# Results of a chunk kept in one piece of TensorE's order, between the halves of the next chunk's scores

## The chip, the cores and the metric

The kernel runs on one core of a Trainium2 chip. The metric is the device time of one execution in microseconds; lower is better. Before the change the median of three runs is 552.49 us (552.18 to 552.93).

Names of the engines in the profile: PE is TensorE (PEld its loading of weights), DVE is VectorE, ACT is ScalarE, POOL is GpSimd, SP issues most of the transfers. All of them run their own list of instructions in order and wait for each other by semaphores.

## What is computed

A gated linear recurrence with a complex decay for each of 4 x 8 heads (768 steps, head dimension 48), then a mixture of eight experts, one expert for each of the 3072 rows:

```python
for t in range(S):                                   # S = 768
    ar, ai = a_re_n[:, :, t, :, None], a_im_n[:, :, t, :, None]
    new_re = ar * S_re - ai * S_im
    new_im = ar * S_im + ai * S_re
    kv = np.einsum('bhd,bhe->bhde', k[:, :, t], v[:, :, t])
    S_re, S_im = new_re + kv, new_im
    y[:, :, t] = np.einsum('bhd,bhde->bhe', q[:, :, t], S_re)
# [...] x = y as (3072, 384) rows
expert_idx = np.argmax(x @ w_gate, axis=1)
# [...] gate weight by softmax; rows sorted by expert
h = np.maximum(x_sorted[lo:hi] @ w1[e], 0.0)         # 384 -> 1024
y_sorted[lo:hi] = h @ w2[e]                          # 1024 -> 384
```

## The kernel before

The recurrence is done in chunks of 128 steps: one chunk `g` is 128 steps of all eight heads of one batch entry, so there are 24 chunks, four (the batch entries `b`) for each of six stretches `s` of the sequence. Two chunks form a unit `u`. For each unit the decays are summed along the steps by a matmul with a triangle (`csl` for the logarithm of the magnitude, `cst` for the angle), turned into factors on ScalarE and VectorE, and multiplied into q and k. Real and imaginary part stand side by side, so q and k of a head have 96 columns. Then, for each chunk:

- `tp`: TensorE transposes q and k, four heads at a time; copies bring them to SBUF as `qt` and `kt`.
- `at`: the scores k times q, 128 x 128 for each head, four heads in one PSUM bank; VectorE multiplies them with the triangle into `am`.
- `dk`: k times v, what the chunk adds to the state.
- `y`: the results, v with the scores plus the state `G` with q. Heads come in pairs: `z = 0` writes partitions 0 to 63, `z = 1` partitions 64 to 127.
- `tpx`, `lt`, `lp`: the results are transposed back and the router's logits are made from them.

```python
psT = ...tile_pool(name="psT", bufs=2, space=PSUM)   # tp
psA = ...tile_pool(name="psA", bufs=1, space=PSUM)   # at
psY = ...tile_pool(name="psY", bufs=1, space=PSUM)   # y
# [...]
def scores(g):

    u, c = divmod(g, U)
    s, b = divmod(g, B)
    Q, K = rotated(u, c, "Q"), rotated(u, c, "K")      # VectorE
    qts, ats = [], []
    for hg in range(H // 4):
        kq = []
        for nm, X in (("qt", Q), ("kt", K)):
            tp = psT.tile([P, 4, P], FP, tag="tp", name="tp")
            for j in range(4):
                nc.tensor.transpose(out=tp[0:DD, j], in_=X[:, hg * 4 + j], identity=ident)
            t = ch.tile([P, 4, P], FP, tag=nm, name=nm, bufs=4 if nm == "qt" else 2)
            copy(nm == "qt" or hg == 1, t[0:DD], tp[0:DD])   # True: ScalarE, False: VectorE
            kq.append(t)
        at = psA.tile([P, 4, P], FP, tag="at", name="at")
        for j in range(4):
            mm(at[:, j], kq[1][0:DD, j], kq[0][0:DD, j])
        am = ch.tile([P, 4, P], FP, tag="am", name="am", bufs=4)
        nc.vector.tensor_tensor(out=am, in0=at, in1=bc(tri, 1, 4), op=OP.mult)
        # [...]
    if s < CB - 1:
        dk = psD.tile([P, H, D], FP, tag="dk", padded_shape=[P, 8, 64], name="dk")
        for h in range(H):
            mm(dk[0:DD, h], K[:, h], T["v", u][:, c, h, 0:D])

def outputs(g):
    # [...]
    y = psY.tile([P, HP, P], FP, tag="y", name="y")
    for i in range(HP):
        for z in range(2):
            hg, j = divmod(2 * i + z, 4)
            mm(y[z * DP : (z + 1) * DP, i], V[:, 2 * i + z], ats[hg][:, j], True, s == 0)
        if s > 0:
            for z in range(2):
                hg, j = divmod(2 * i + z, 4)
                mm(y[z * DP : (z + 1) * DP, i], G[0:DD, 2 * i + z], qts[hg][0:DD, j], False, True)
    # [...] state: t = dk + G on VectorE, G = t * M once in four chunks
    xt = xl.tile([P, HP, P], FP, tag="xt", name="xt")
    nc.scalar.copy(out=xt, in_=y)
    tp = psB.tile([P, HP, 2, DP], FP, tag="tp", name="tpx")
    for i in range(HP):
        nc.tensor.transpose(out=tp[:, i].rearrange("p z d -> p (z d)"), in_=xt[:, i], identity=ident)
    # [...] copy to x on ScalarE
    logits(xt, g)                                      # lt, copy ls, lp, copy lg
```

The loop, with the decay steps of the next unit left out:

```python
for u in range(NU + 1):
    # [...] loads; decay_steps, decay_sums (csl), angle_sums (cst), rotation (CS)
    for c in range(U):
        g = (u - 1) * U + c
        if g >= 0:
            scores(g)
        if u < NU:
            decayed(u, c)
        if g > 0:
            outputs(g - 1)
        # [...] routing of chunks that are done
```

The order of this text is not the order on the engines. A scheduler places each instruction, within what data and buffers allow; only instructions tied with `queue(...)` keep their order for certain. In `before` nothing ties the matmuls of the chunks. All matmuls work in f32; TensorE takes each in two passes, which the trace records as two instructions.

After the 24th chunk the expert part begins: for each expert `hps` (384 to 1024) and `yps` (1024 to 384), with the weights loaded ahead.

Of the kernel before, what the change touches and what calls it, by code (L numbers as in the profile page):

```python
# [10 lines left out]
FP = mybir.dt.float32  # L11
# [3 lines left out]
OP = mybir.AluOpType  # L15
# [5 lines left out]
P = 128  # L21
# [8 lines left out]
def bc(ap, axis, n):  # L30

    shape = list(ap.shape)
    shape.insert(axis, n)
    return ap[tuple([slice(None)] * axis + [None])].to_broadcast(shape)
# [3 lines left out]
def kernel(  # L38
# [12 lines left out]
    nc = tc.nc  # L51
    B, H, S, D = q.shape
    DD = 2 * D
# [4 lines left out]
    NT = N // P  # L58
    CB = S // P
    U = 2  # L60
# [14 lines left out]
    DP = 64  # L75
    HP = H // 2
# [3 lines left out]
    def mm(o, lhsT, rhs, start=True, stop=True):  # L80
        return nc.tensor.matmul(o, lhsT=lhsT, rhs=rhs, start=start, stop=stop, skip_group_check=True)  # L81

    def copy(i, o, in_):
        (nc.scalar.copy if i % 2 else nc.vector.tensor_copy)(out=o, in_=in_)  # L84
# [7 lines left out]
    def const(shape, name, dt=FP):  # L92
        return cp.tile(shape, dt, name=name)

    ident = const([P, P], "ident")
    make_identity(nc, ident)
    tri = const([P, P], "tri")
# [21 lines left out]
    gbuf = [const([P, H, DP], f"G{i}") for i in range(B)]  # L119
# [39 lines left out]
    T, W_T = {"put": []}, {}  # L159

    def queue(ins, before):

        tc.add_manual_dep(ins.ins, before.ins.name, NOSYNC, reason="queue order")
        return ins
# [55 lines left out]
    ch = att.enter_context(tc.tile_pool(name="ch", bufs=2))  # L220
    psM = att.enter_context(tc.tile_pool(name="psM", bufs=1, space=PSUM))
    psT = att.enter_context(tc.tile_pool(name="psT", bufs=2, space=PSUM))
    psA = att.enter_context(tc.tile_pool(name="psA", bufs=1, space=PSUM))
    psY = att.enter_context(tc.tile_pool(name="psY", bufs=1, space=PSUM))
    psB = att.enter_context(tc.tile_pool(name="psB", bufs=1, space=PSUM))
    psD = att.enter_context(tc.tile_pool(name="psD", bufs=1, space=PSUM))
# [47 lines left out]
    def load_a(u):  # L274
        load(u, (("ar", a_re), ("ai", a_im)))
# [131 lines left out]
    def rotated(u, c, nm):  # L407
        t = ch.tile([P, H, 2, D], FP, tag=nm, name=nm)
        e = bc(T.pop((nm, u, c)), 2, 2)
        nc.vector.tensor_tensor(out=t, in0=T["CS", u][:, c * H : (c + 1) * H], in1=e, op=OP.mult)  # L410
        return t.rearrange("p h a d -> p h (a d)")
# [78 lines left out]

        return [lambda i=i: put(i) for i in range(n)] + ([last] if end else [])

    def scores(g):

        u, c = divmod(g, U)
        s, b = divmod(g, B)
        Q, K = rotated(u, c, "Q"), rotated(u, c, "K")
        qts, ats = [], []
        for hg in range(H // 4):
            kq = []  # L500
            for nm, X in (("qt", Q), ("kt", K)):
                tp = psT.tile([P, 4, P], FP, tag="tp", name="tp")
                for j in range(4):
                    nc.tensor.transpose(out=tp[0:DD, j], in_=X[:, hg * 4 + j], identity=ident)  # L504
                t = ch.tile([P, 4, P], FP, tag=nm, name=nm, bufs=4 if nm == "qt" else 2)
                copy(nm == "qt" or hg == 1, t[0:DD], tp[0:DD])
                kq.append(t)
            at = psA.tile([P, 4, P], FP, tag="at", name="at")
            for j in range(4):
                mm(at[:, j], kq[1][0:DD, j], kq[0][0:DD, j])  # L510
            am = ch.tile([P, 4, P], FP, tag="am", name="am", bufs=4)
            nc.vector.tensor_tensor(out=am, in0=at, in1=bc(tri, 1, 4), op=OP.mult)  # L512
            qts.append(kq[0])
            ats.append(am)
        if s < CB - 1:
            dk = psD.tile([P, H, D], FP, tag="dk", padded_shape=[P, 8, 64], name="dk")
            for h in range(H):
                mm(dk[0:DD, h], K[:, h], T["v", u][:, c, h, 0:D])
            T["dk", g] = dk
        T["s", g] = qts, ats  # L520

    def outputs(g):

        u, c = divmod(g, U)
        s, b = divmod(g, B)
        qts, ats = T.pop(("s", g))
        V, G = T["v", u][:, c], gbuf[b]
        y = psY.tile([P, HP, P], FP, tag="y", name="y")
        for i in range(HP):
            for z in range(2):  # L530
                hg, j = divmod(2 * i + z, 4)
                mm(y[z * DP : (z + 1) * DP, i], V[:, 2 * i + z], ats[hg][:, j], True, s == 0)
            if s > 0:
                for z in range(2):
                    hg, j = divmod(2 * i + z, 4)
                    mm(y[z * DP : (z + 1) * DP, i], G[0:DD, 2 * i + z], qts[hg][0:DD, j], False, True)
        if s < CB - 1:
            t = ch.tile([P, H, D], FP, tag="t", name="t")
            if s == 0:
                nc.scalar.copy(out=t[0:DD], in_=T["dk", g][0:DD])  # L540
            else:
                nc.vector.tensor_tensor(out=t[0:DD], in0=T["dk", g][0:DD], in1=G[0:DD, :, 0:D], op=OP.add)
            if b == B - 1:
                decay_total(s)
            T["t", b] = t
            if b == B - 1:
                for i in range(B):
                    M = bc(T["M", s][0:DD, i], 2, D)
                    (nc.vector.tensor_tensor(out=gbuf[i][0:DD, :, 0:D], in0=T["t", i][0:DD], in1=M, op=OP.mult))
# [5 lines that stand above are left out]
        if b == 0:  # L555
            T["x", g] = T["x"] = xl.tile([P, GR, XW], FP, tag="x", name="x", bufs=3)
        T["copied"] = nc.scalar.copy(
            out=T["x"][:, b, :DM].rearrange("p (i z d) -> p i z d", z=2, d=D), in_=tp[:, :, :, 0:D]
        )
        logits(xt, g)  # L560
# [24 lines left out]
    for z in range(2):  # L585
        nc.sync.dma_start(
            out=wg[z * DP : z * DP + D, :, 0:E],
            in_=w_gate.rearrange("(i z d) e -> z d i e", z=2, d=D)[z],
# [14 lines left out]
    for u in range(NU + 1):  # L603
        if 0 < u < NU:
            load_qkv(u)
        for i in range(NS // (P * BL)):
            if 2 + i * 2 // (NS // (P * BL)) == u:
                blank(i)

        if u < NU:  # L610
            steps = decay_steps(u + 1)[0] if u + 1 < NU else []
            own = [lambda c=c: decay_sums(u, c) for c in range(U)]
            if u == 0:
                steps = steps[:2] + own + steps[2:]
            else:
                steps = steps[:1] + own[:1] + steps[1:3] + own[1:] + steps[3:]
            table("natural_log_exp_and_others")
            for i, f in enumerate(steps):
                f()
                if i == 1:  # L620
                    carry_angle(u)
            for f in T.pop("chosen", []):
                f()
            for c in range(U):
                angle_sums(u, c)
            table("trig_and_small")
            if 0 < u < NU - 1:
                decay_angle(u + 1)
            rotation(u)
            if u == 0:  # L630
                decay_angle(1)
            if u == NU - 1:
                while T["put"]:
                    place()
                experts_at(range(1), True)
                load_w(0, range(KD + KF // 2))
                own0 = gather(0, 0, [P] * (FIRST // P))
        if u < NU:
            place()
        for f in T.pop("route", []):  # L640
            T["put"] += f()
        for c in range(U):
            g = (u - 1) * U + c
            if g >= 0:
                scores(g)
            if u < NU:
                decayed(u, c)
            if g > 0:
                outputs(g - 1)

            n = {NT - GR: GR, NT - U: U}.get(g)
            if n:
                if n == GR:
                    queue(table("natural_log_exp_and_others"), T["copied"])
                choose(g - n, n)()
                T["put"] += route(g - n, n)
                while T["put"]:
                    place()
        for _ in range(2 if u >= NU - 2 else 1):
            place()  # L660
        if u > 2 and u % 2 and u < NU - 1:

            j = (u - 3) * U
            T["chosen"] = [choose(j, GR)]
            T["route"] = [lambda j=j: route(j, GR)]
        if u + 2 < NU:
            load_a(u + 2)
    outputs(NT - 1)
    choose(NT - U, U)()
    for f in route(NT - U, U):  # L670
# [343 lines left out]
```

## Time and profile before

| | before |
|---|---|
| time, median of three | 552.49 us |
| span of the profiled execution | 551.8 us |
| TensorE busy | 535.6 us (97%) |
| VectorE busy | 272.0 us (49%) |
| ScalarE busy | 279.7 us (51%) |
| GpSimd busy | 128.5 us (23%) |
| read from and written to HBM | 63.3 and 15.5 MB, 143 GB/s |

The page gives busy time over the whole span, and then the span in 40 slices of 13.8 us, one digit each (tenths of the slice). Chunks run up to about 278 us, which is slice 20; what follows is the expert part. For what happens inside the first half three other views are used: stages of 20 us, the waits of one engine (who waited for whom, total, times, longest), and the timeline, where each line is a group of neighbouring instructions with start, length, engine, line of the code, output and inputs, and the number of records. Neighbouring matmuls overlap in the timeline, so the length of a group is longer than the time to the next group's start.

The costs of the instructions concerned, from the groups between 0 and 320 us (number of records, mean length of one):

| instruction | records | mean |
|---|---|---|
| `at`, TensorE | 384 | 286 ns |
| `y` from `am` and v, TensorE | 384 | 288 ns |
| `y` from `qt` and G, TensorE | 320 | 280 ns |
| `tp` of q and of k, TensorE | 192 each | 285, 283 ns |
| `dk`, TensorE | 320 | 252 ns |
| copy to `qt`, ScalarE | 48 | 581 ns |
| copy to `kt`, VectorE / ScalarE | 24 / 24 | 683 / 581 ns |
| `am`, VectorE | 48 | 687 ns |
| `xt`, ScalarE | 24 | 587 ns |

### The profile page before, as it was taken

What the parts mean: (1) busy time and instruction counts of PE and PEld (TensorE: products, weight loads), DVE (VectorE), ACT (ScalarE), POOL (GpSimd) and SP (SyncE); (2) the same over time, 40 slices, a digit from 0 to 9 for tenths busy, and PEclk for the clock granted to TensorE, in tenths of its full rate; (3) what the DMA queues carried; (4) which work ended last, traced back from release to release, by engine and by line L of the source; (5) the groups of instructions that cost most, each with busy time, mean ns of one, the idle gap of its engine ahead of it and who ended that gap; (6) DMA issues with size and microseconds to landing.
All of it is one profiled execution on the core that took longest, in us unless ns stands there. A gap on an engine that the chain in (4) does not pass through costs nothing.

```text
span 551.8 us, 8779 instructions
## 1 busy us (share of the span) xinstructions
PE 535.6 (97%) x3310; PEld 369.7 (67%) x3310; DVE 272.0 (49%) x640; ACT 279.7 (51%) x473; POOL 128.5 (23%) x148
## 2 busy tenths in 40 slices
PE   8899999999999999999999999999999999999995
PEld 6777688778778878778776655555555555565553
DVE  3757788978888887877551212121404032210110
ACT  7867877877776886744310112534343351615200
POOL 2110111141241140210222000605234160514301
PEclk9959999999999999999999999999999999999998
DMA  9999954918754633461114996472944819370001
GB/s 186 187 259 236 262 94 88 182 52 145 129 131 88 121 84 58 105 224 18 43 44 113 309 359 160 136 194 121 281 137 163 240 47 280 128 255 15 25 4 42
DMA packets 163566, 79.32 MB, mean 144 GB/s; under 512 B 144896, under 2 KB 156861, under 8 KB 162619
## 3 DMA queue, kind: packets, MB, share of 16 engines
q1 hardware_dynamic: 158651, 69.04, 51.6%
q0 software_dynamic: 4864, 9.63, 5.0%
q8 instruction: 28, 0.46, 0.4%
q14 instruction: 23, 0.19, 0.1%
HBM read 63.30 MB, written 15.46 MB: 143 GB/s over the span
## 4 chain that ended last, share of the span: by engine, by line
PE 84%; DMA 6%; DVE 3%; ACT 3%; issue 3%; SPq 0%; POOL 0%; POOLq 0%; DVEq 0%; ACTq 0%
PE hps L81 23%; PE yps L81 22%; PE y L81 9%; PE at L81 7%; PE tp L504 7%; PE dk L81 5%; PE cst L81 3%; PE csl L81 3%; DMA ai<-in_a_im_dram 2%; PE tpx L554 2%; DMA xs<-x,slot 1%; PE lt L81 1%; DMA ai<-c 1%; DMA c<-ai 1%; ACT R L230 1%
## 5 line engine op out<-in xcount | busy, mean ns | idle before, releaser
L81 PE MATMUL yps<-w2t,ht 128*128 128x384 f32 (+6 forms) x464 | 135.1, 487 | 0.0
L81 PE MATMUL hps<-xt,w1t 128*128 128x256 f32 (+8 forms) x432 | 133.9, 469 | 0.3 <-DVE xt L708 0.3
L81 PEld LDWEIGHTS hps<-xt,w1t 128*128 128x128 f32 x432 | 80.0, 190 | 52.8 <-issue 25.2
L81 PEld LDWEIGHTS yps<-w2t,ht 128*128 128x128 f32 (+6 forms) x464 | 75.8, 177 | 56.8 <-issue 6.9
L742 ACT ACTIVATE ht<-hps 128x256 f32<-128x256 f32 (+8 forms) x36 | 17.0, 472 | 118.5 <-PE hps L81 117.5
L759 DVE TENSOR_SCALAR y<-yps,gi 128x384 f32<-128x384 f32 (+2 forms) x24 | 14.7, 615 | 107.6 <-PE yps L81 107.6
L722 POOL DMA_INDIRECT out_dram<-y,gi x29 | 28.2, 974 | 122.6 <-DVE y L759 86.5
L81 PE MATMUL at<-qt,kt 96*128 96x128 f32 x384 | 54.9, 286 | 0.9 <-DVE kt L84 0.9
L746 DVE TENSOR_SCALAR ht<-hps 128x256 f32<-128x256 f32 (+8 forms) x36 | 19.2, 532 | 70.9 <-PE hps L81 70.8
L81 PEld LDWEIGHTS at<-qt,kt 96*128 96x128 f32 x384 | 48.7, 196 | 6.5 <-DVE kt L84 1.4
L81 PE MATMUL y<-am,v 128*64 128x128 f32 x384 | 52.8, 288 | 0.0
L81 PE MATMUL y<-qt,G 96*64 96x128 f32 x320 | 45.5, 280 | 0.0
L482 POOL DMA_INDIRECT xs<-x,slot x24 | 24.8, 1035 | 86.2 <-DMA xs<-x,slot 39.8
L81 PEld LDWEIGHTS y<-am,v 128*64 128x64 f32 x384 | 32.7, 137 | 13.7 <-issue 12.3
L512 DVE TENSOR_TENSOR am<-at,tri 128x512 f32<-128x512 f32 x48 | 33.0, 687 | 13.9 <-PE at L81 13.4
L84 ACT COPY qt<-tp 96x512 f32<-96x512 f32 x48 | 27.9, 581 | 15.1 <-PE tp L504 15.0
L242 ACT ACT_TABLE_LOAD x27 | 34.6, 1283 | 1.2 <-PEq L1000 0.8
L504 PE MATMUL tp<-ident,Q 128*96 128x128 f32 x192 | 32.5, 285 | 2.0 <-DVE Q L410 2.0
L800 POOL TENSOR_TENSOR cs<-cs,cw 128x768 f32<-128x768 f32 x12 | 21.7, 1809 | 50.7 <-ACT cw L796 50.7
L81 PEld LDWEIGHTS dk<-v,K 128*96 128x96 f32 x320 | 31.4, 170 | 3.0 <-issue 1.9
L504 PE MATMUL tp<-ident,K 128*96 128x128 f32 x192 | 32.5, 283 | 0.7 <-DVE K L410 0.7
L81 PEld LDWEIGHTS y<-qt,G 96*64 96x64 f32 x320 | 30.9, 136 | 3.2 <-issue 2.6
(140 smaller groups left out, 752.8 us busy)
## 6 DMA issues: line engine op xcount, KB each, us to landing
w1t<-in_moe_w_dram SPq DMA_DIRECT2D x7, 1536.0 KB, 7.1
w2t<-in_moe_w_dram SPq DMA_DIRECT2D x7, 1536.0 KB, 7.5
xs<-zrow SPq DMA_DIRECT2D x7, 772.0 KB, 10.3
q<-in_q_dram SPq DMA_DIRECT2D x12, 384.0 KB, 5.3
k<-in_k_dram SPq DMA_DIRECT2D x12, 384.0 KB, 5.5
v<-in_v_dram SPq DMA_DIRECT2D x12, 384.0 KB, 4.3
car<-in_a_re_dram SPq DMA_DIRECT2D x12, 384.0 KB, 8.3
cai<-in_a_im_dram SPq DMA_DIRECT2D x12, 384.0 KB, 9.2
```

Of the source, the lines that this page charges most:

```text
L81: return nc.tensor.matmul(o, lhsT=lhsT, rhs=rhs, start=start, stop=stop, skip_group_check=True)
L84: (nc.scalar.copy if i % 2 else nc.vector.tensor_copy)(out=o, in_=in_)
L242: ins = nc.scalar.preload_act_table_set(name)
L482: pool(nc.gpsimd.indirect_dma_start(out=xs[:, :], out_offset=bass.IndirectOffsetOnAxis(ap=to[:, i : i + 1], axis=0), in_=x[:, i], in_offse ...
L504: nc.tensor.transpose(out=tp[0:DD, j], in_=X[:, hg * 4 + j], identity=ident)
L512: nc.vector.tensor_tensor(out=am, in0=at, in1=bc(tri, 1, 4), op=OP.mult)
L554: nc.tensor.transpose(out=tp[:, i].rearrange("p z d -> p (z d)"), in_=xt[:, i], identity=ident)
L722: T["out"] = nc.gpsimd.indirect_dma_start(out=out, out_offset=bass.IndirectOffsetOnAxis(ap=idx, axis=0), in_=y[0:m], in_offset=None, bound ...
L742: relu = nc.scalar.activation(out=ht[:, f], in_=ps, func=AF.Relu)
L746: nc.vector.tensor_scalar(out=ht[:, f], in0=ps, scalar1=0.0, scalar2=None, op0=OP.max)
L759: nc.vector.tensor_scalar(out=y[0:m], in0=ps[0:m], scalar1=gate, scalar2=None, op0=OP.mult)
L800: nc.gpsimd.tensor_tensor(out=s, in0=s, in1=w, op=OP.add)
```

## The change

No instruction of the computation is added or taken away. `scores` and `outputs` are cut into smaller functions, and their transposes, score matmuls and results (not `dk`, `csl`, `cst`, `tpx`, `lt`, `lp`) are tied to one another by the function `pe`, so that they stand on TensorE in the order of the text: all four groups of transposes of chunk g, the first half of its scores, all results of chunk g - 1, the second half of the scores of g. The purpose is that the 64-column matmuls of the results follow one another without other shapes between, while the second half of the scores gives ScalarE the time to copy the results out, and the results give VectorE the time to free the one bank of the scores.

```diff
-    def scores(g):
+    def pe(ins):
+
+        if "pe" in T:
+            queue(ins, T["pe"])
+        T["pe"] = ins
+
+    def turned(g, hg):
+
+        u, c = divmod(g, U)
+        if hg == 0:
+            T["QK", g] = rotated(u, c, "Q"), rotated(u, c, "K")
+        kq = []
+        for nm, X in zip(("qt", "kt"), T["QK", g]):
+            tp = psT.tile([P, 4, P], FP, tag="tp", name="tp")
+            for j in range(4):
+                pe(nc.tensor.transpose(out=tp[0:DD, j], in_=X[:, hg * 4 + j], identity=ident))
+            t = ch.tile([P, 4, P], FP, tag=nm, name=nm, bufs=4 if nm == "qt" else 2)
+            copy(nm == "qt" or hg == 1, t[0:DD], tp[0:DD])
+            kq.append(t)
+        T["kq", g, hg] = kq
+
+    def scores(g, hg):
+
+        qt, kt = T["kq", g, hg]
+        at = psA.tile([P, 4, P], FP, tag="at", name="at")
+        for j in range(4):
+            pe(mm(at[:, j], kt[0:DD, j], qt[0:DD, j]))
+        am = ch.tile([P, 4, P], FP, tag="am", name="am", bufs=4)
+        nc.vector.tensor_tensor(out=am, in0=at, in1=bc(tri, 1, 4), op=OP.mult)
+        T["am", g, hg] = am
+
+    def update(g):
+        # [...] dk as before, not tied
+
+    def results(g, hg):
 
         u, c = divmod(g, U)
         s, b = divmod(g, B)
# [...]
+        V, G = T["v", u][:, c], gbuf[b]
+        if hg == 0:
+            T["y"] = psY.tile([P, HP, P], FP, tag="y", name="y")
+        y, am, qt = T["y"], T["am", g, hg], T["kq", g, hg][0]
+        for i in range(2):
+            for z in range(2):
+                o = y[z * DP : (z + 1) * DP, 2 * hg + i]
+                pe(mm(o, V[:, 4 * hg + 2 * i + z], am[:, 2 * i + z], True, s == 0))
+            if s > 0:
+                for z in range(2):
+                    o = y[z * DP : (z + 1) * DP, 2 * hg + i]
+                    pe(mm(o, G[0:DD, 4 * hg + 2 * i + z], qt[0:DD, 2 * i + z], False, True))
# [...]
             if g >= 0:
-                scores(g)
+                turned(g, 0)
+                turned(g, 1)
+                scores(g, 0)
+                update(g)
+            if g > 0:
+                for hg in range(H // 4):
+                    results(g - 1, hg)
+            if g >= 0:
+                scores(g, 1)
             if u < NU:
                 decayed(u, c)
             if g > 0:
# [...] outputs(g - 1) without the results
+    for hg in range(H // 4):
+        results(NT - 1, hg)
     outputs(NT - 1)
```

More of the change, by code (lines that the diff above doesn't have):

```diff
@@ new lines, in scores @@
+    def scores(g, hg):
[7 more added lines that the diff above has]
+    def update(g):
+        u, c = divmod(g, U)
+        if g // B < CB - 1:
+            dk = psD.tile([P, H, D], FP, tag="dk", padded_shape=[P, 8, 64], name="dk")
+            for h in range(H):
+                mm(dk[0:DD, h], T["QK", g][1][:, h], T["v", u][:, c, h, 0:D])
+            T["dk", g] = dk
@@ L495, in scores @@
+    def results(g, hg):
         u, c = divmod(g, U)
         s, b = divmod(g, B)
[L497 to L520, printed above, removed]
+        V, G = T["v", u][:, c], gbuf[b]
[10 more added lines that the diff above has]
+                    pe(mm(o, G[0:DD, 4 * hg + 2 * i + z], qt[0:DD, 2 * i + z], False, True))
@@ L525, in outputs @@
         s, b = divmod(g, B)
[L526 to L536, printed above, removed]
+        y, G = T["y"], gbuf[b]
         if s < CB - 1:
```

## The prediction

> **What bounds the kernel now.** I read four views: the page (busy shares and slices), the table of twenty-microsecond stages, TensorE's own waits, and TensorE's timeline. The page first:
>
> ```profile
> PE 535.6 (97%) x3310; PEld 369.7 (67%) x3310; DVE 272.0 (49%) x640; ACT 279.7 (51%) x473; POOL 128.5 (23%) x148
> ...
> PE   8899999999999999999999999999999999999995
> ...
> DVE  3757788978888887877551212121404032210110
> ACT  7867877877776886744310112534343351615200
> ...
> PEclk9959999999999999999999999999999999999998
> ```
>
> TensorE (PE) is in use in every slice. The attention part is the first half: there VectorE (DVE) and ScalarE (ACT) stand at 7 to 8 tenths; afterwards, in the expert part, they are light. The change touches the attention part alone. One slice near the start has the slow clock. The stage table puts numbers on it (columns: stretch, its length, then busy time and instruction count of PE, PEld, DVE, ACT, POOL, then clock, DMA share, GB/s):
>
> ```profile
> 80.00:100.00 20.00, 20.00 (x188) 15.68 (x185) 16.27 (x40) 14.46 (x24) 2.75 (x5) 1.00 0.52 94
> 120.00:140.00 20.00, 20.00 (x199) 16.88 (x196) 16.76 (x43) 14.68 (x24) 2.70 (x5) 1.00 0.60 106
> sum 180.00, PE 177.13 PEld 139.51 DVE 149.74 ACT 138.74 POOL 39.00; mean PE 19.68 PEld 15.50 DVE 16.64 ACT 15.42 POOL 4.33
> ```
>
> Two chunks take about 20 us. From 60 to 240 us DVE works 149.74 of 180 us, 83%, ACT 77%: next in line, but not the bound. DMA is half used once the first 80 us are over. And TensorE hardly waits for anybody:
>
> ```profile
> PE tpx L554 <- ACT xt L551: 2.0, 5, 0.7
> PE tp L504 <- DVE Q L410: 2.0, 2, 1.8
> ...
> PE at L81 <- DVE kt L84: 0.9, 2, 0.5
> ```
>
> All its waits in that view come to 10 us in the whole run; in the starts of its instructions I find about 6 us of waiting between 40 and 280 us. So the attention part lasts as long as TensorE needs to get through its list, and a shorter list shortens the run. How long the list is can't be read from busy time, because neighbouring matmuls overlap in it; I take it from starts (columns: start in us, length in us, ... x records; a matmul in f32 makes two records, a transpose one):
>
> ```profile
> 126.17 0.60 PE L504 MATMUL tp<-ident,K 128*96 128x128 f32 x4
> 126.61 0.60 PE L504 MATMUL tp<-ident,Q 128*96 128x128 f32 x4
> 127.05 1.31 PE L81 MATMUL dk<-v,K 128*96 128x48 f32 x14
> ...
> 132.54 0.60 PE L504 MATMUL tp<-ident,K 128*96 128x128 f32 x4
> 133.07 0.44 PE L81 MATMUL y<-am,v 128*64 128x128 f32 x4
> 133.34 0.38 PE L81 MATMUL y<-qt,G 96*64 96x128 f32 x2
> 133.66 0.19 PE L81 MATMUL rps<-oh,tri_x 128*128 128x32 bf16 x1
> ...
> 145.15 0.64 PE L504 MATMUL tp<-ident,Q 128*96 128x128 f32 x4
> 145.72 0.43 PE L81 MATMUL y<-qt,G 96*64 96x128 f32 x2
> 146.09 0.91 PE L81 MATMUL csl<-A,tri_half 128*128 128x384 f32 x2
> ```
>
> Four transposes followed by transposes or dk last 0.44 us (126.17 to 126.61 to 127.05), 0.109 each. Followed by a result (y) they last 0.53 (132.54 to 133.07). Preceded and followed by results they last 0.57 (145.15 to 145.72). One lone result takes 0.37 us (145.72 to 146.09). Three take 0.59 (133.07 to 133.66). Going into and out of the y matmuls costs something, and in the kernel before it is paid often.
>
> [...] The y matmuls use 64 columns (128*64 in the list), lt uses 32, all others 96 or 128[...]. [...] from the start of a transpose to the next instruction's start it is 109 ns if that is a transpose, 202 ns if it is y. [...] Here the two halves z=0 and z=1 start 6 to 7 ns apart (median of all such pairs 7), so a pair costs one pass and an unpaired y as much as a pair. [...] The trace has 213 ns per record from 30 to 39 us, against 109 to 112 later. This start-up stage I leave as it is.
>
> **The change part by part.** All instructions stay: 352 results, 384 transposes, 192 score matmuls, 160 for dk, as many copies. What changes is their order. I fitted all 81 pieces of results in the trace before: a piece of n pairs lasts, from its first start to the first start after it, 0.149 + 0.216 n us (measured 0.363 and 0.370 for one pair, 0.583 and 0.589 for two, 1.03 for four, 1.25 for five). In the compiled orders the results stand in 81 pieces before and in 35 after (not 24, since the scheduler still puts dk, cst or csl inside some). Then:
>
> 1. Fixed part of a piece: 46 fewer by 0.149 = 6.9 us.
> 2. Way in: 93 ns (202 - 109). Before, 7 of the 81 follow lt, whose own way out has paid; after, 1 of 35. So 74 - 34 = 40 by 0.093 = 3.7 us.
> 3. Slots for pairs: 46 of the 81 pieces have an odd number of results, 22 of the 35; the slots fall from 199 to 187. 12 by 0.216 = 2.6 us.
> 4. First record after a piece: a transpose there takes 151 ns and not 109 (20 cases before, none after), dk 35 ns more (7 and 5), a score matmul 213 and not 112 (18 before, 20 after). Before 20 x 0.042 + 7 x 0.035 + 18 x 0.101 = 2.9, after 5 x 0.035 + 20 x 0.101 = 2.2. Gain 0.7 us.
>
> Sum: 13.9 us off a list that sets the end. Against it:
>
> 5. The four groups of transposes of a chunk now stand together and have two PSUM buffers. From the last start of a group to the end of its copy the trace has 0.89 us at least (ACT, 0.58 of it the copy), 0.99 typically on DVE; with 0.07 to wake TensorE the third group can't start before 0.96. In 18 of 24 chunks the new order puts csl, cst, dk or lt between. In 6 only lp or the small rps stands there: the gap is 0.55 to 0.69 and 0.3 to 0.5 us are lost in each. 6 x 0.45 = 2.7 us. The old order had none of these.
> 6. The copy xt of the results must end before tpx. In the new order a half of the scores (0.9 us) mostly stands between, which just covers the 0.89 us; but ACT may be in an 0.8 to 0.9 us activation when y ends. Before, these waits cost 2.0 us; I add 0.5. One lp follows its lt directly: 0.4.
> 7. DVE and ACT have the same work in less time: 16.6 us in each 20 become 16.6 in 18.9, 88%. Results served as movable filling when a copy was late; now they are fixed between two halves of scores. Chosen, not derived: 1 us of waits more, as half of the score matmuls wait for a copy on the DVE.
>
> 13.9 - 2.7 - 0.9 - 1.0 = 9.3 us, so 552.5 - 9.3 = 543.2; I say 543.0. The expert part moves forward as a whole: its weights for the first expert are asked for before attention ends, and DMA is half idle there.
>
> **The rivals.** (a) [...] The order is now a chain of transposes, scores, results. If ACT is late with one copy (a quarter of the qt copies start 1.5 us or more after their transposes), nothing else may be left to run. For it: DVE at 83% already, and the loss of the filling. Against: the new order still has dk (1.36 us a chunk), csl and cst (0.75 each) to move about, and before, with the same two engines, only 6 us in 240 were lost. At 0.35 us a chunk more it costs 8 us and the run stays at 550 to 552; only at over 0.6 us a chunk is it slower than before.
> (b) [...] no wait of 5 to 7 shows, because the scheduler set the order with the copies in view. Then 552.5 - 13.9 = 538.6.
> (c) Attention is paced by something that TensorE hides: loads, or the chain of activations on ACT for the next unit. Then nothing moves, 551 to 553. The first 70 us have DMA at 9 tenths, and 2 or 3 us of the gain may be lost there. Against it for the rest: ACT 77% and DMA near half, and TensorE without idle time.
>
> **Range and chances.** The centre is the sum. The range 538.0 to 549.5 goes from (b), with a little more, to a case in which rival (a) eats three fifths of the gain. Two per cent is 541.4, 1.6 us below my value. I give 0.35 to that, 0.60 to within 2%, and 0.05 to slower by over 2%, which would need over 24 us of new waits.
>
> **What would show it.** Right: y pieces of 16 lasting about 1.88 us (0.149 + 8 x 0.216); the stretch from 60 to 240 us in the old trace run through some 8 us faster; TensorE's waits grown, with tp behind qt and kt copies as a new line of about 3 us; busy time of DVE and ACT unchanged. Step 7 wrong: waits for kt, am or Q of together over 6 us. The prediction fails if the pieces still cost 0.37 us a pair, or if the sum of TensorE's waits in attention exceeds 15 us.

## The result, and the profile after

The changed kernel takes 559.53 us (median of four runs, 558.40 to 561.18), against 552.67 before in the same comparison: ratio 1.0128, interval 1.0096 to 1.0159. It is slower by 1.3%, where 543.0 us and a gain were predicted. The page of the changed kernel, in its lines for the engine totals, TensorE's slices and TensorE's clock:

```profile
PE 528.1 (95%) x3310; PEld 372.0 (67%) x3310; DVE 271.3 (49%) x640; ACT 280.4 (50%) x473; POOL 133.1 (24%) x148
...
PE   8897699999899999989999999999999999999995
...
PEclk9887979999999999989999999999999999999999
```

TensorE is in use for 7.5 us less than before (535.6), so the list did become shorter, and yet the span grew from 551.8 to 556.4 us. Most of the lost time is in slices 3 and 4 of the second line (counted from 0; 42 to 70 us), which stood at 9 before, and in the clock: it is reduced in slices 1, 2, 3, 5 and 17, where before only slice 2 was (and the last). Half clock (0.50 in the trace) was granted in the profiled execution before for 13.7 us from 25.8 us; after for 6.8 us from 24.9, 6.8 from 48.8, 6.8 from 69.2 and 3.4 from 246.7 us (in both also at the very end). TensorE's waits in the changed kernel (who waited for whom, total, times, longest):

```profile
PE tp L508 <- DVE Q L410: 4.9, 2, 3.1
PE at L81 <- DVE am L521: 4.2, 1, 4.2
PE cst L81 <- ACT qt L84: 2.5, 1, 2.5
```

Three long stops, not many short ones (the 4.9 us are two, 3.1 and, at the start of the kernel, 1.8). Half clock follows each of them: at the second it begins 1.0 us before the stop ends, at the first and the third 1.5 and 1.3 us after. In the third line `qt` is not what cst waited for: that copy had ended 0.75 us earlier. The carried angle, which cst reads, landed at 245.31 us, 0.09 us before cst started. The pieces of results themselves are as predicted. In TensorE's timeline a whole piece, from its first y to the first score matmul after it (239.05 - 237.14), takes 1.91 us:

```profile
237.14 0.44 PE L81 MATMUL y<-am,v 128*64 128x128 f32 x4
...
238.73 0.39 PE L81 MATMUL y<-qt,G 96*64 96x128 f32 x4
239.05 1.16 PE L81 MATMUL at<-qt,kt 96*128 96x128 f32 x8
```

So where do the stops come from? The timeline of all engines at the first one, in the changed kernel (in brackets: idle time of the engine before, and what ended it):

```profile
43.74 0.42 PE L81 MATMUL lt<-xt,wg 128*32 128x128 f32 x8
...
46.22 0.16 DVE L327 SCALAR_TENSOR_TENSOR c<-fl,c 96x8 f32<-96x8 f32 x1 [4.87 <-DMA c<-ai]
46.30 0.95 DVE L410 TENSOR_TENSOR Q<-CS,Qe 128x768 f32<-128x768 f32 x1
...
47.17 0.68 DVE L521 TENSOR_TENSOR am<-at,tri 128x512 f32<-128x512 f32 x1
47.30 0.64 PE L508 MATMUL tp<-ident,Q 128*96 128x128 f32 x4 [3.14 <-DVE Q L410]
...
49.65 2.69 PE L81 MATMUL dk<-v,K 128*96 128x48 f32 x16
```

`c` is an addition on 96 x 8 numbers: it carries the angle from one stretch of the sequence to the next. Its input comes by a transfer of 3 KB which GpSimd issued at 38.83 us, while the input loads kept all DMA engines busy (a DMA share of 1.09 from 38.8 to 46.2 us). The addition took 0.16 us, but VectorE had stood still for 4.87 us before it, with Q and am behind it in its list; the scores that am reads were done at 42.73 us, and am started at 47.17. TensorE ran out of anything else at 44.16 us and stood still until Q came. From 48.8 us its clock was halved: 16 records of dk take 2.69 us at 49.65, where 16 take 1.48 us at full clock (before, at 41.10 us). The second stop is the same, at the next unit:

```profile
64.95 1.09 PE L81 MATMUL y<-am,v 128*64 128x128 f32 x16
...
69.36 0.16 DVE L327 SCALAR_TENSOR_TENSOR c<-fl,c 96x8 f32<-96x8 f32 x1 [4.71 <-DMA c<-ai]
69.45 0.68 DVE L521 TENSOR_TENSOR am<-at,tri 128x512 f32<-128x512 f32 x1
...
70.28 0.98 PE L81 MATMUL at<-qt,kt 96*128 96x128 f32 x3 [4.23 <-DVE am L521]
```

The kernel before has this wait too. There the timeline at that moment reads:

```profile
43.36 1.06 PE L81 MATMUL at<-qt,kt 96*128 96x128 f32 x8
...
45.80 0.91 PE L81 MATMUL csl<-A,tri_half 128*128 128x384 f32 x2
46.64 0.66 PE L81 MATMUL y<-am,v 128*64 128x128 f32 x8
47.23 1.16 PE L81 MATMUL at<-qt,kt 96*128 96x128 f32 x8
47.62 0.16 DVE L327 SCALAR_TENSOR_TENSOR c<-fl,c 96x8 f32<-96x8 f32 x1 [2.47 <-DMA c<-ai]
47.70 0.95 DVE L410 TENSOR_TENSOR Q<-CS,Qe 128x768 f32<-128x768 f32 x1
```

The transfer is just as late (c starts at 47.62 us), and Q stands behind c here too. But am and kt were done ahead of c on VectorE, and TensorE had scores, a csl and half of a chunk's results to do meanwhile: it waited 0.20 us for Q and not 3.14. Two things differ, then: what stands behind c, and what TensorE has left to do until c is done.

The third stop, 2.5 us, is at cst. GpSimd's timeline shows why the carried angle came late, again in the changed kernel:

```profile
235.09 4.18 POOL L482 DMA_INDIRECT xs<-x,slot  x1 [1.98 <-DMA xs<-x,slot]
239.25 0.59 POOL L330 DMA_DIRECT2D ai<-c  x1
```

c was done at 236.26 us, but the transfer back (ai) stood behind a scatter of rows that held GpSimd for 4.18 us. The transfer itself then took 6.06 us (3.5 in the median of the ten), beside the load of the first expert's weights, asked for from 236.27 us on. TensorE's cst could start at 245.40 only.

### The profile page after: what moved, and what is told of

It is laid out like the page before. It is cut to its first block, busy times and chain, and to the rows that moved or that the text cites. A ratio compares the mean times of both kernels' runs of the same rounds, so it can differ in the third digit from the quotient of the medians.

```text
span 556.4 us, 8788 instructions
## 1 busy us (share of the span) xinstructions
PE 528.1 (95%) x3310; PEld 372.0 (67%) x3310; DVE 271.3 (49%) x640; ACT 280.4 (50%) x473; POOL 133.1 (24%) x148
## 4 chain that ended last, share of the span: by engine, by line
PE 85%; ACT 5%; DVE 3%; DMA 3%; issue 2%; POOL 0%; SPq 0%; POOLq 0%; DVEq 0%; ACTq 0%
PE yps L81 24%; PE hps L81 24%; PE y L81 8%; PE at L81 7%; PE tp L508 7%; PE dk L81 5%; PE csl L81 3%; PE cst L81 3%; DMA c<-ai 3%; PE tpx L572 2%; ACT L242 1%; PE lt L81 1%; ACT R L230 1%; PE lp L81 1%; DMA ar<-in_a_re_dram 1%
## 5 line engine op out<-in xcount | busy, mean ns | idle before, releaser
L81 PEld LDWEIGHTS hps<-xt,w1t 128*128 128x128 f32 x432 | 80.1, 190 | 52.2 <-issue 25.8
L81 PE MATMUL at<-qt,kt 96*128 96x128 f32 x384 | 56.1, 287 | 4.5 <-DVE am L521 4.2
L482 POOL DMA_INDIRECT xs<-x,slot x24 | 29.7, 1237 | 74.0 <-DMA xs<-x,slot 32.4
L81 PE MATMUL y<-am,v 128*64 128x128 f32 x384 | 41.4, 279 | 0.0
L81 PE MATMUL y<-qt,G 96*64 96x128 f32 x320 | 35.3, 273 | 0.0
L81 PE MATMUL dk<-v,K 128*96 128x48 f32 x320 | 32.9, 255 | 0.7 <-DVE t L560 0.7
L508 PEld LDWEIGHTS tp<-ident,Q 128*96 128x96 f32 x192 | 22.0, 137 | 14.4 <-DVE Q L410 6.2
```

The lines of the kernel that those rows point to most:

```text
L482: pool(nc.gpsimd.indirect_dma_start(out=xs[:, :], out_offset=bass.IndirectOffsetOnAxis(ap=to[:, i : i + 1], axis=0), in_=x[:, i], in_offse ...
L508: pe(nc.tensor.transpose(out=tp[0:DD, j], in_=X[:, hg * 4 + j], identity=ident))
```

## The experiments

Theory 1: the loss is one small wait at the head of an engine's list, c on VectorE (and the transfer back on GpSimd for the third stop), with half clock as a consequence; apart from it the changed order gains what was predicted. Theory 2, my own rival (a): the fixed order takes away filling everywhere, so that late copies stop TensorE.

**c on GpSimd, in the changed kernel and in the one before.**

```diff
-            nc.vector.scalar_tensor_tensor(
-                out=c0, in0=T["fl", u - B // U], scalar=2.0 * math.pi, in1=c0, op0=OP.mult, op1=OP.add
-            )
+            fl = T["fl", u - B // U]
+            nc.gpsimd.tensor_scalar(out=fl, in0=fl, scalar1=2.0 * math.pi, scalar2=None, op0=OP.mult)
+            nc.gpsimd.tensor_tensor(out=c0, in0=fl, in1=c0, op=OP.add)
```

Changed kernel: 

> The changed kernel with one thing moved: the small addition that carries the angle from one stretch to the next (c) is done by GpSimd (two instructions) and not by VectorE. In the changed kernel VectorE stood still for 4.9 and 4.7 us at c, waiting for a small transfer, with am and Q behind it, and TensorE stood still behind those. Theory 1 (that wait in VectorE's list is the loss, and the slow clock that follows it): the loss of about 13 us up to the eighth slice goes away, 542 to 548 us. Theory 2 (the fixed order loses its filling everywhere, copies come late): 556 to 560 us, as the changed kernel.

Kernel before: 

> The kernel before with the same move of c to GpSimd. There VectorE waited at c for 4.2 us in all, and TensorE stood still for under 1 us behind it. Theory 1: little to win, 549 to 553 us, so that the changed order is faster by some 1% once c is out of VectorE's list. Theory 2: 549 to 553 us too, and the changed order stays slower than this.

Measured: 540.90 us for the changed kernel (ratio to before 0.9798, interval 0.9728 to 0.9867) and 549.52 us for the one before (0.9943, 0.9924 to 0.9962). The first is 18.6 us faster than the changed kernel by moving 10 additions of 0.15 us to an engine with nothing urgent behind them; it is 1 us below what theory 1 expected. The second wins 0.6%. The move of c lets the scheduler order TensorE anew: 37 pieces (35 in the changed kernel) and 82 (81 before). The new order is 8.6 us faster than the old. The page of the changed kernel with c on GpSimd, TensorE's slices and clock:

```profile
PE   8798999999999999899999999999999999999995
...
PEclk9989999999999999999999999999999999999999
```

Half clock is left only near the start and at the very end, and the first two stops are gone. The timeline shows that the transfer was no faster:

```profile
44.95 1.48 PE L81 MATMUL dk<-v,K 128*96 128x48 f32 x16
...
46.03 2.54 POOL L329 TENSOR_TENSOR c<-fl,c 96x8 f32<-96x8 f32 x1 [5.74 <-DMA c<-ai]
...
46.27 0.88 PE L81 MATMUL csl<-A,tri_half 128*128 128x384 f32 x2
46.98 0.60 PE L508 MATMUL tp<-ident,Q 128*96 128x128 f32 x4
...
52.62 0.88 PE L81 MATMUL cst<-ai,tri_turn 128*128 128x384 f32 x2 [2.27 <-issue]
```

GpSimd waits 5.74 us for it and the addition comes at 46.03 us, as late as before; VectorE and TensorE go on. One stop remains, 2.27 us at cst, whose carried angle GpSimd sent back at 48.87 us. No half clock followed it.

**The carry left out.** `carry_angle` returns at once: no c, no transfers to it and back. The later stretches then have other angles, so this computes less than the reference.

Changed kernel: 

> The changed kernel with the carry of the angle left out altogether (no c, no transfer to it and back to ai; the angles of later stretches start from nothing, so the output is another one). Its order on TensorE is that of after_c_pool (540.9 us), so the difference to it is what the carry still costs once it is out of VectorE's list. Theory 1: the wait was in VectorE's list, 538 to 541 us. Rival (the slow transfer itself paces the unit, through cst): several us below after_c_pool, 532 to 537.

Kernel before: 

> The kernel before with the carry of the angle left out in the same way; its order on TensorE is that of before_c_pool (549.5 us). Theory 1: 547 to 550 us, so that the changed order is some 8.5 us faster with the carry gone too. Rival (slow transfer paces the unit): clearly below, 540 to 546.

Measured: 539.68 us (0.9783, 0.9767 to 0.9799) and 548.31 us (0.9948, 0.9930 to 0.9965). TensorE's order is, record for record, that of the kernels with c on GpSimd. Both times are 1.2 us lower, but the kernel before was 0.5 us lower too in this comparison (551.94 against 552.45), and the ratios agree within their intervals. In the trace the stop at cst falls from 2.3 to 0.8 us. So the slow transfer is not what paces the units; it hurt through what stood behind it. The gain of the order is 8.6 us again. Here both profiled executions have 6.8 us of half clock near the start; in the pair with c on GpSimd it was 3.4 with the new order and 6.8 with the old, so the pair without the carry is the cleaner one.

**The third stop.** `pool` ties scatters to one another in the order of the text; here the transfer back to ai is tied among them, and two scatters near the end are asked for later:

```diff
-            nc.gpsimd.dma_start(out=T["th", u][0:1].rearrange(...), in_=c0)
+            pool(nc.gpsimd.dma_start(out=T["th", u][0:1].rearrange(...), in_=c0))
...
-        for _ in range(2 if u >= NU - 2 else 1):
+        for _ in range(0 if u == NU - 2 else 2 if u > NU - 2 else 1):
             place()
```

> The changed kernel with c left on VectorE, but with the scatter of rows (xs) tied behind the transfer that brings the carried angle back (ai), on GpSimd's list, and two scatters near the end of attention moved behind it. TensorE's order is that of the changed kernel but for a few instructions of the last chunks. Only the third stop, 2.5 us at 243 us with 3.4 us of slow clock after it, had that transfer held up by a 4.2 us scatter. If that is its cause: the stop goes, and the first two (behind c on VectorE) stay: 554 to 557 us. If the weights' load alone slows it: 558 to 561 us.

Measured: 554.12 us (1.0024, 1.0005 to 1.0043), 5.4 us less than the changed kernel. The wait at cst is gone and so is the half clock at 247 us, with the weights asked for at the same time as before (236.6 us); the first two stops are there as before, 2.4 and 4.4 us. The transfer back went out at 237.14 us and not at 239.25, and took 4.8 us. So the scatter in front made the stop; how much of the delay was the transfer's own slowness beside the weights, no run separates.

An earlier try at it missed its aim:

```diff
-                experts_at(range(1), True)
-                load_w(0, range(KD + KF // 2))
-                own0 = gather(0, 0, [P] * (FIRST // P))
...
+        if u == NU - 1:
+                experts_at(range(1), True)
+                load_w(0, range(KD + KF // 2))
+                own0 = gather(0, 0, [P] * (FIRST // P))
```

> The changed kernel with the load of the first expert's weights and rows asked for two chunks later, after the last transfer of the carry and not beside it. In the changed kernel TensorE stood still for 2.5 us at 243 us, at cst, which reads the carried angle, and had the slow clock for 3.4 us after it. If the weights' load slows that small transfer: these 4 us go, 554 to 557 us. If not: 558 to 561 us.

Measured: 569.98 us (1.0345, 1.0318 to 1.0371). The scheduler left the weights' load where it was (236.35 us) and the stop at cst stayed at 2.7 us, so the question was not asked. Only the rows of the first expert came later, and the expert part began with a wait of 4.5 us for them and 10.2 us of half clock. This says nothing for or against either theory.

**Fewer ties.** In one kernel the matmuls of the first six chunks are free (`if "pe" in T and T["tie"]`, with `T["tie"] = g >= 6` ahead of each chunk), in the other only the results are tied, to one another (`pe(...)` taken off the transposes and the score matmuls).

> The changed kernel, but the matmuls of the first six chunks are not tied (the time in which loads keep the transfers slow); from the seventh on they are. Theory 1: the early stops go, the later chunks keep their gain of about 0.45 us each, 544 to 549 us. Theory 2: most chunks are still tied, 555 to 560 us.

> The results are tied to one another alone; transposes and scores are free. In the compiled order the results then stand in 76 pieces, against 81 before and 35 in the changed kernel. Theory 1: [...] no stops made, 550 to 554 us. Theory 2 (the tie between transposes and scores is what hurts): the same. Slower than 555 would say that the order among the results is the loss.

Measured: 549.60 us (0.9941, 0.9909 to 0.9973) and 557.18 us (1.0076, 1.0052 to 1.0099). Both are slower than theory 1 said, the second by over 3 us, which I had set down as a sign against the order among the results. Their traces say why: c stopped them too. With the first six chunks free, TensorE still stood 2.2 us for Q at 45 us, 1.2 us for am at 64, and 2.8 us at cst at 232 us with 6.8 us of half clock. With only the results tied it stood 2.6 us for Q and 3.1 us at cst. So the full set of ties is not needed to bring TensorE to a stop behind c: these two other orders stop there as well. That c could have stayed on VectorE, further down its list, was not tried. The results-only kernel was then built with c on GpSimd as well:

> results_only (557.2 us) with c done by GpSimd. It has 75 pieces of results, about as many as before. Theory 1 (it was slower than before through stops at c, as its trace shows slow clock at 48 and 243 us): as before_c_pool, 547 to 551 us. Rival (tying the results costs by itself): 554 to 558 us.

Measured: 546.26 us (0.9902, 0.9885 to 0.9918), 10.9 us less, with 75 pieces. It is 3.3 us faster than the kernel before with c on GpSimd (2.3 by the ratios), which theory 1 didn't promise. TensorE's list of waits from 40 us to the end of attention has 1.9 us, against 3.2 there; the rest of the difference stays open.

**One tie more.** With c on GpSimd, dk is tied as well, behind the second half of the scores (`pe(mm(dk...))`, and `update(g)` moved there), so that no dk breaks a piece:

> after_c_pool (540.9 us), and in addition dk is tied too, behind the second half of the scores, so that it stands in no piece of results any more: in the compiled order 29 pieces (17 of them whole) against 37, 181 slots against 189. Theory 1 (pieces cost 0.149 us each and 0.093 on the way in, a slot 0.216): 8 x 0.242 + 8 x 0.216 = 3.7 us less, 536 to 539 us. Theory 2 (every tie takes filling away): dk is the last movable work between the transposes, waits grow by more, 541 to 546 us.

Measured: 564.03 us (1.0178, 1.0120 to 1.0236). This is slower than either theory said, in the direction of theory 2. The 17 whole pieces still take 1.91 us each, but TensorE now stops where it waits for VectorE and finds nothing else to run. TensorE's waits, and the clock line of the page:

```profile
PE cst L81 <- DVE f L381: 8.0, 7, 2.2
PE dk L81 <- ACT t L558: 2.2, 1, 2.2
...
PEclk9989889989969979988999999999999999999998
```

The sums have one PSUM buffer, and the second cst of a unit waits until VectorE has read the first (f). Half clock is granted for 37 us in all after the start (10.2, 3.4, 10.2, 6.8 and 6.8). Half of that, 19 us, comes close to all TensorE's waits in the list together, 22.8 us. The edit both ties dk and moves it behind the second half of the scores; no run tells the two apart.

## Why the prediction was wrong

**Steps 1 to 4, the list of TensorE: right.** 35 pieces were found in the trace; the way in was 93 ns; a score matmul after a piece took 213 ns, dk 35 ns more; a whole piece 1.91 us, predicted 1.88. What in TensorE takes the 93 ns and the fixed 149 ns of a piece, no run shows; the steps rest on the fitted times alone.

**Steps 5 to 7, short waits: right in sum once the long ones are away, but by luck in the parts.** For the orders with c on GpSimd or without the carry (37 and 82 pieces), steps 1 to 4 give 13.1 us. 8.6 were measured, so waits and slower steps took some 4.5; predicted 2.7 + 0.9 + 1.0 = 4.6. TensorE's list of waits from 40 us to the end of attention (it leaves out those under 0.15 us) accounts for only a part: without the carry it has 4.9 us with the new order and 3.4 with the old. Transposes waiting for copies (step 5) are 1.1 us of the 4.9, where 2.7 were expected. Where step 5 has 0.07 us to wake TensorE, the changed kernel's trace has 0.054 us from the end of a copy to the transposes that waited for it (at 264.36 us), 0.94 us after the last start of the group copied, not 0.96. Step 6 had its sign wrong for tpx, where one wait of 0.7 us is left of 2.0, and lp behind lt costs 1.3 us and not 0.4. In the changed kernel itself, the 15 chunks from 83.4 us to 239.2 us (starts of the copies xt) take 155.8 us, and took 162.7: 0.46 us a chunk gained, predicted 9.3 / 24 = 0.39.

**What failed is step 7, with the reading it stood on.** It put new waits at 1 us, "chosen, not derived", and reasoned with VectorE's load of 88%. In the changed kernel the new waits are three stops of together 10.5 us, with half clock after them that costs, by estimate, about 8 more. The sign set down for step 7 (waits for kt, am or Q of together over 6 us) came true: 1.0 + 4.2 + 4.9 = 10.1 us, of which 1.8, at the start, were there before. The waits that mattered do not come from VectorE's load: it stood idle in the first two. I had read TensorE's waits alone, and from "TensorE hardly waits for anybody" concluded that nothing slow stood near. In the profile before, VectorE's own list has 4.2 us for c behind its transfer, in two pieces, at the same two units, and TensorE's list has a short form of the third stop (at 239.6 us):

```profile
DVE c L327 <- DMA c<-ai: 4.2, 2, 2.5
PE cst L81 <- DMA ai<-c: 0.8, 1, 0.8
```

Rival (c) named loads in the first 70 us, but as something that hides a gain, not as something that the new order exposes.

**The size.** The three stops are 3.1 + 0.7 (the second wait, for K, belongs to the first stop), 4.2 and 2.5 us, together 10.5. Half clock after them: 6.8 us from 48.8 and 3.4 us from 246.7, all of it at work, and from 69.2 to 76.0 us at work since 70.28. At a clock of 0.50, half of these is lost: 3.4 + 1.7 + 2.9 = 8.0 us. At the start, half clock lasts 6.8 us and not 13.7, which gives back about 3.4; but its length there changes from run to run (6.8 us in the profiled kernel before with c on GpSimd), so this term need not belong to the change. 552.7 - 9.3 + 10.5 + 8.0 - 3.4 = 558.5, and 561.9 without it; measured 559.5. The two larger terms after the gain were in no step of the prediction. That the half clock costs 8.0 is an estimate from its length; no run took it away while leaving the stops. The criterion named in advance, TensorE's waits in attention above 15 us, was met.

**Rival (a)** was half right. That nothing else may be left to run is what the stops show; but what came late was no copy of ScalarE, it was c behind its transfer, and away from it the order gains 0.46 us a chunk. The limit set there, 0.6 us a chunk, is also too high: on top of the predicted sum, 9.3 / 24 = 0.39 us a chunk is enough to lose the gain. The stops and the half clock come to 18.5 / 24 = 0.77. With dk tied and moved, the loss of filling takes the whole gain and more.

## What to carry to other kernels

Before pinning an order on the engine that is the bound, read the waits of the engines that feed it: here c, waiting for a transfer at the head of VectorE's list, held back everything behind it for 4.87 and 4.71 us, and a wait that looked harmless before (TensorE waited 0.20 us for Q) became the critical path (3.14 us) once TensorE had lost its filling. Put such an instruction on an engine that has nothing urgent, before or together with the change of order: here that alone turned a loss of 1.3% into a gain of 2.0%. Pin what has to stay together and leave the rest movable: with c on GpSimd the results, transposes and scores could be pinned with a gain (540.9 us), and pinning dk as well, behind the scores, lost it (564.0 us).

## What the runs showed of the hardware

- Stops of TensorE of 2.2 to 2.8 us were followed by half clock of 3.4 to 10.2 us in several places (2.5 us at 243 in the changed kernel; 2.2 us at 156 and at 203 with dk tied), and so were three stops of 0.5 to 0.8 us between 112 and 116 us there. But two stops of the same length had no half clock after them: 2.3 us at 50 us in the changed kernel with c on GpSimd, and 2.2 us at 45 us with the first six chunks free. So the length of one stop does not decide it in these runs. Where half clock came, it began before the stop ended or up to 1.5 us after it, and in the changed kernel it cost nearly as much again as the stops (8.0 and 10.5 us, the 8.0 an estimate).
- An indirect scatter that mostly holds GpSimd for 1.0 us (the median of 24) held it for 4.2 us at 235 us in the changed kernel, and the small transfer behind it, ready at 236.3, went out at 239.25 us.
